# HGRN2 attention and FNet mixing on one core: the up-projection of three batches as fifteen block products in place of eighteen

## The chip, the cores and the metric

The kernel runs on one core of one Trainium2 chip. The core has five engines with an instruction queue each, which work side by side and wait for one another by semaphores: PE (TensorE, the matmuls; its weight loads are listed apart as PEld), DVE (VectorE), ACT (ScalarE), POOL (GpSimd) and SP (SyncE, which here only issues DMAs). Matmul results land in PSUM, which has eight banks; a bank holds 512 fp32 columns on 128 partitions. Everything else is in SBUF.

The metric is the device time of one execution in microseconds, lower is better. The time given is a median over several executions. A profile is one execution more, with the hardware profiler on.

## What is computed

The reference has two parts. The first is a gated linear recurrence over 768 steps for each of 4 batches and 8 heads with 48 channels. Its output `x` is a 768 x 384 matrix for each batch. The second part mixes it and applies a two-layer network:

```python
state = f[:, :, t, :, None] * state + np.einsum('bhd,bhe->bhde', k[:, :, t], v[:, :, t])
y[:, :, t] = np.einsum('bhd,bhde->bhe', q[:, :, t], state)
...
X = np.fft.fft(x, axis=1)
X = np.fft.fft(X, axis=2)
u = x + np.real(X)
mu = np.mean(u, axis=-1, keepdims=True)
var = np.mean((u - mu) ** 2, axis=-1, keepdims=True)
un = (u - mu) / np.sqrt(var + 1e-06)
ch = np.maximum(un @ w_ch1, 0.0) @ w_ch2
return u + ch
```

`w_ch1` is 384 x 1536 and `w_ch2` is 1536 x 384. The product `un @ w_ch1` is called the up-projection here, the product with `w_ch2` the down-projection. All matmuls of both are fp32.

## The kernel before

**Order of the work.** The order is written out by hand. `ORDER` (lines 27 to 47) is a string of words, and the loop at the end of the kernel issues one step for each word, so every engine's queue gets its instructions in the order of the words. A number `n` is the next step of attention unit `n`. There are 16 units, one for each pair of heads: units 0 to 3 belong to batch 0, and so on. `Ln` with letters loads a unit's f, k, q or v. `Kn` transposes a unit's keys. `Fb` is the next step of batch `b`'s Fourier mixing. `Hb` is the next step of its normalization and transposes. `Pb` is the next step of its two projections. `r` fetches a block of the weights, `C` converts it to fp32. `W` combines blocks of `w_ch2`. `V` and `c` read the weights a second time and look at their sizes. `D` are matmuls on constants during the start, and `M` computes a flag at the end. If that flag is set, a second and slower path computes everything again. With these inputs it isn't taken.

**Attention.** A unit's f, k and q (112 partitions x 768) live in one of four `g` tiles, one of three `k` tiles and one of four `q` tiles, picked by the unit's number (`u % 4`, `u % 3`, `u % 4`). A unit's steps are: two activations (lines 331, 332), a scan on DVE (338), exponentials (342 to 346), two products on DVE (350, 351), matmuls into a PSUM tile `sc` (359), a masked copy (363), matmuls into `y` (517), a second `sc` tile (534), state differences `ds` (557), a scan (565), matmuls into `y` (574), copies, transposes `yt` (594), and additions and subtractions on DVE that prepare the Fourier mixing, the fold (621 to 627). All these short-lived PSUM tiles come from the pool `ps_a`, which has two buffers of two banks each.

**Mixing and normalization.** `fnet` makes `z` (683) and `mix` (702), adds `mix` to `x` and takes the moments on DVE (line 758 and following). `turn` normalizes a tile of 128 tokens (738), transposes it on PE (741) and copies it to `unT` on ACT (742).

**Projections.** `projected` handles a batch in three pairs of token tiles. For each pair, `unT` holds 384 channels of two tiles of 128 tokens. The up-projection computes 12 blocks of 128 hidden channels. Each is three matmuls (one for each 128 channels, line 783) with 128 x 128 weights and 256 moving columns, the two token tiles side by side, into a buffer of the PSUM pool `ps_f`. ACT then applies the ReLU into `h` (785). `h` is kept in two tiles of six blocks each, from a pool `ph1` of two buffers. The down-projection then takes seven products of six matmuls each (806) in place of eight, with sums of `h` formed on DVE (813 to 824) and its results added to `x` on DVE (817 to 840). The first pair of batch 0 uses a plain down-projection (792), because the weights' combinations aren't ready by then. A step of `Pb` is one block of the up-projection or one of the seven products, so a pair takes 20 steps.

Of the kernel before, what the change touches and what calls it, by code (L numbers as in the profile page):

```python
# [12 lines left out]
C = 128  # L13
# [11 lines left out]


ORDER = (
    "L0f Z L1f I 0 D D L0q D 0 i D 1 1 D 0 L2f L0k 0 D D D r L0v D D C L1q D 2 D L2k 0 D L1k D 1 0 2 1 r "
    "0 L2q K0 C L3fk 0 D 0 1 2 D 1 2 3 0 3 2 2 L4fk L1v 4 K1 r 1 4 C 1 1 L3q 3 0 1 L2v K2 3 r 2 L3v 1 0 3 "
    "C 2 L5fk 3 D 5 D D 2 4 L4qv 2 R K3 2 3 1 D 3 4 2 3 4 3 2 5 L5qv 4 3 L7fk T 5 4 3 S K4 7 D 3 L6fk C r "  # L30
    "4 4 C F0 r F0 F0 5 F0 C 4 F0 K5 5 H0 5 H0 C r 4 5 H0 L7qv C r C r r F0 L6qv 6 F0 5 C P0 6 C P0 P0 P0 "
    "5 r 6 P0 P0 5 6 C 6 K6 r C P0 r H0 C 6 r P0 P0 P0 7 r C P0 6 r H0 C r P0 6 C 7 H0 r P0 C r 7 6 C r C "
    "P0 7 6 7 K7 r P0 L9fk L8qv C L9qv 7 C 6 L8fk C 7 5 P0 9 4 5 9 P0 P0 7 8 P0 P0 9 P0 P0 8 8 L10fk P0 9 "
    "7 9 L10qv K9 H0 P0 P0 8 P0 9 P0 P0 P0 9 8 9 H0 9 L11fk P0 W P0 9 K8 8 10 P0 11 10 P0 11 8 7 P0 8 6 "
    "11 P0 P0 P0 6 L11qv P0 11 P0 P0 8 10 P0 P0 7 P0 P0 P0 7 F1 F1 L13qv P0 F1 10 L13fk K10 F1 P0 10 10 8 "
    "L12fk F1 P0 10 11 L14fk H1 H1 P0 P0 12 F1 P0 10 H1 P0 P0 14 P0 P0 L12qv 10 12 P0 P0 12 P0 P0 P0 P1 "
    "P1 12 9 P1 P1 F1 11 10 K11 P1 P1 P1 H1 P1 P1 11 12 11 H1 P1 L15fk 11 13 P1 P1 14 10 11 8 13 13 H1 8 "
    "12 P1 P1 P1 P1 P1 10 P1 P1 P1 P1 P1 P1 11 9 K12 P1 13 10 P1 P1 P1 P1 P1 V P1 P1 H1 11 12 13 11 12 H1 "
    "P1 F2 12 F2 14 P1 P1 P1 P1 13 15 L14qv P1 P1 12 K13 P1 P1 F2 F2 P1 P1 14 13 14 F2 P1 13 H2 13 P1 V "
    "15 14 P1 P1 P1 P1 L15qv P1 H2 P1 P1 13 H2 F2 P1 15 14 K14 F2 P1 P1 P1 V P1 P1 P1 15 P1 P1 P2 H2 P2 "  # L40
    "P2 c V P2 c c P2 P2 P2 V V K15 P2 14 12 P2 P2 14 14 15 H2 P2 V c P2 15 c 12 15 14 P2 15 H2 P2 P2 15 "
    "13 c P2 P2 14 P2 c P2 H2 V 15 P2 H2 P2 P2 P2 13 14 V P2 P2 15 P2 V 15 15 P2 P2 P2 F3 P2 c F3 P2 F3 "
    "F3 P2 F3 F3 P2 F3 c c P2 P2 P2 P2 P2 P2 P2 P2 P2 V P2 P2 c P2 P2 P2 V c P2 H3 V P2 P2 H3 H3 P2 P2 P2 "
    "P2 P2 P2 P2 P2 P2 P2 P3 P3 P3 V V P3 V H3 c H3 V P3 P3 P3 c P3 c V c c V P3 H3 P3 P3 P3 P3 P3 V P3 c "
    "P3 V V c P3 V P3 c P3 P3 P3 c P3 P3 P3 P3 P3 H3 H3 P3 P3 P3 c P3 P3 P3 P3 P3 V P3 P3 P3 P3 P3 P3 P3 "
    "P3 P3 P3 c P3 P3 P3 c M P3 P3 P3 P3 P3 P3 P3 P3 P3 P3 P3 P3 P3"
)

PAIRS = ((0, 3), (2, 5), (1, 4))
LAST_PAIRS = ((2, 5), (1, 4), (3, 0))  # L50
# [3 lines left out]
def kernel(  # L54
# [32 lines left out]
    p2 = ctx.enter_context(tc.tile_pool(name="p2", bufs=2))  # L87
    pr = ctx.enter_context(tc.tile_pool(name="pr", bufs=3))
    p3 = ctx.enter_context(tc.tile_pool(name="p3", bufs=4))
    ph1 = ctx.enter_context(tc.tile_pool(name="ph1", bufs=2))  # L90
    ps_a = ctx.enter_context(tc.tile_pool(name="ps_a", bufs=2, space=bass.MemoryType.PSUM))
    ps_y = ctx.enter_context(tc.tile_pool(name="ps_y", bufs=1, space=bass.MemoryType.PSUM))
    ps_f = ctx.enter_context(tc.tile_pool(name="ps_f", bufs=2, space=bass.MemoryType.PSUM))
# [6 lines left out]

    nc.scalar.preload_act_table_set("natural_log_exp_and_others")

    g_t = [fixed([128, S + 1], f"g{i}") for i in range(4)]
    k_t = [fixed([128, S], f"k{i}") for i in range(3)]
    q_t = [fixed([128, S], f"q{i}") for i in range(4)]
    at_t = [fixed([128, 2, NCH, 64], f"at{i}") for i in range(2)]
    ao_t = [fixed([128, 2, NCH // 2, 64], f"ao{i}") for i in range(2)]
    causal = fixed([128, C], "causal")
# [48 lines left out]
    def load(u, *names):  # L157
        if u >= B * HP:
            return
        b, hp = divmod(u, HP)  # L160
        for name in names:
            if name == "v":
                v_of[u] = (p3.tile([128, NCH, 2 * D], F32, tag="v", name=f"v{u}"),
                           pr.tile([128, NCH // 2, 2 * D], F32, tag="vx", name=f"vx{u}"))
                nc.sync.dma_start(out=v_of[u][0], in_=v[b, hp])
                nc.sync.dma_start(out=v_of[u][1][64:], in_=v[b, hp, :64, 3:])
                continue
            t, i = {"f": (g_t[u % 4], 2), "k": (k_t[u % 3], 1), "q": (q_t[u % 4], 0)}[name]
            rows = qkf.rearrange("b h r d i s -> (b h r d) i s")
            first = 2 * D * u  # L170
            nc.sync.dma_start(out=t[:2 * D, :S], in_=rows[first:first + 2 * D, i])
            nc.sync.dma_start(out=t[2 * D:R, :S], in_=rows[first + D:first + 64, i])
# [116 lines left out]

    def reread():  # L290
        i = len(second)
        t = (k_t[1], g_t[1], k_t[2], g_t[2])[i % 4][:, :S].bitcast(U32)
        _, src, cols = blocks_of[i]
        if wide:
            nc.sync.dma_start(out=t, in_=src.bitcast(U32)[:, 2 * cols.start:2 * cols.stop])
        second.append(t.rearrange("p (n w) -> p n w", w=2))
# [27 lines left out]
    def attention(u, x_all):  # L324
# [1 line left out]

        Q, K, g = q_t[u % 4][:R], k_t[u % 3][:R], g_t[u % 4][:R, :S]
        AT, AO = at_t[u % 2], ao_t[u % 2]  # L330
        nc.scalar.activation(g, g, AF.Exp, scale=-1.0, accum_out=hot[:R, u:u + 1])
        nc.scalar.activation(g, g, AF.Ln, bias=1.0)  # L332
# [3 lines left out]
        T = deep[:R, u]  # L336
        W = p2.tile([128, S], F32, tag="W", name=f"W{u}")[:R]
        nc.vector.tensor_tensor_scan(W, g, bound[:R], 0.0, ALU.add, ALU.min)  # L338
        nc.vector.tensor_tensor(T, g_t[u % 4][:R, C::C], W[:, C - 1::C], ALU.add)
        yield  # L340

        nc.scalar.activation(g, W, AF.Exp, scale=-1.0)
# [26 lines left out]
    def attention_by_blocks(u, x_all):  # L369
# [2 lines left out]

        Q, K, g = q_t[u % 4][:R], k_t[u % 3][:R], g_t[u % 4][:R, :S]
        AT = ph1.tile([128, 2, NCH, C], F32, tag="h1", name=f"at{u}")
        nc.gpsimd.memset(AT, 0.0)
        masks = causal.rearrange("p (i n) -> p i n", n=32)
        AD = ph1.tile([128, 2, 2 * NCH, 64], F32, tag="h1", name=f"ad{u}")[:, :, :NCH, :32]
        nc.gpsimd.memset(AD, 0.0)  # L380
        mul = nc.vector.tensor_tensor

# [278 lines left out]
    def fnet(b, x):  # L661
# [94 lines left out]
        for c in range(3):  # L756
# [6 lines left out]
                nc.vector.tensor_copy(x[0:1, 3], row[0:1])  # L763
            yield

    def projected(b, x, again=False):


# [3 lines left out]
        for j, (c, d) in enumerate(PAIRS if b < B - 1 else LAST_PAIRS):  # L772
# [1 line left out]
                for _ in range((3, 3, 2)[j] if b < B - 1 else (3, 2, 3)[j]):  # L774
                    next(behind[b], None)
            unT = turned_of[b][j].rearrange("p k t n -> p k (t n)")
            hs = []
            for m in range(NF):
                if m % H == 0:
                    hs.append(ph1.tile([128, H, 2, 128], F32, tag="h1", name=f"h1_{b}_{j}_{m}"))  # L780
                pp = ps_f.tile([128, 512], F32, tag="f", name=f"up{b}_{j}_{m}")
                for kt in range(3):
                    nc.tensor.matmul(pp[:, :256], lhsT=w1[:, kt, m * 128:(m + 1) * 128], rhs=unT[:, kt],  # L783
                                     start=(kt == 0), stop=(kt == 2))
                nc.scalar.activation(hs[-1][:, m % H].rearrange("p t n -> p (t n)"), pp[:, :256], AF.Relu)  # L785
                yield
            if not again and (b, j) == (0, 0):

                for t, i in enumerate((c, d)):
                    po = ps_f.tile([128, 512], F32, tag="f", name=f"po{b}_{i}")  # L790
                    for m in range(NF):
                        nc.tensor.matmul(po[:, :DM], lhsT=hs[m // H][:, m % H, t], rhs=w2[:, m],  # L792
                                         start=(m == 0), stop=(m == NF - 1))
                        if m in (2, 5, 8):
                            yield
                    tt(x[:, i], po[:, :DM], x[:, i], ALU.add)
                    store(b, i, x[:, i])
                    yield
                continue
            h11, h21, h12, h22 = [hs[k][:, :, t] for k in range(2) for t in range(2)]  # L800
            c1, c2, d1, d2 = [x[:, i, o:o + HD] for i in (c, d) for o in (0, HD)]

            def product(i, out, h, start=False):
# [64 lines left out]
    with tc.manual_schedule():  # L868
        for word in ORDER.split():
# [3 lines left out]
                    units[n] = attention(n, lambda b=n // HP: x_all(b))  # L873
                next(units[n], None)
            elif kind == "K":
                keys_turned(n, g_t[n % 4][:R, :S])
            elif kind == "F":
                if n not in fronts:
                    fronts[n], rest[n] = fnet(n, x_of[n]), projected(n, x_of.pop(n))
# [2 lines left out]
                next(rest[n], None)  # L882
            elif kind == "W":
                combine()
            elif kind == "H":
                next(behind[n], None)
            elif kind == "r":
                fetch()
            elif kind == "V":
                reread()  # L890
            elif kind == "D":
                busy()
            elif kind == "C":
                weights()
            elif kind == "c":
                sizes()
            elif kind == "R":
                fetch(3)
            elif kind == "L":
                load(n, *word.strip("L0123456789"))  # L900
            elif kind == "I":
                start()
            elif kind == "i":
                nc.sync.dma_start(out=ident, in_=ident_in)
            elif kind == "T":
                wave = tables()
            elif kind == "S":
                sort_tables(wave)
            elif kind == "Z":
                zeros()  # L910
            elif kind == "M":
                flag = judge()
    tc.no_sync_barrier()
    again = nc.values_load(flag[0:1, 0:1], min_val=0, max_val=1)
    with tc.If(again > 0):
        if wide:
            for i, (dst, _, _) in enumerate(blocks_of):
# [86 lines left out]
```

## Time and profile before

| | |
|---|---|
| median of 3 executions | 542.58 us (542.5 to 543.71) |
| the profiled execution | 542.37 us |
| its span, from the first instruction to the last | 540.6 us |
| mean granted TensorE clock | 0.983 of full speed |
| PE busy with up-projection matmuls (L783) | 194.4 us, 864 records |
| PE busy with down-projection matmuls (L806), its five groups added | 161.8 us |
| DVE busy, ACT busy | 291.9 us, 201.1 us |
| DMA | 48.07 MB, mean 89 GB/s |

How to read it: an engine's busy time is the time in which at least one of its instructions runs, and "L783" is line 783 of the kernel. An fp32 matmul shows as two records on PE, each with a weight load of its own. Matmuls are pipelined: a record's length includes the way through the array, so the pace of a stream is read from how many records a stretch holds, not from their lengths. A group's line gives busy time and the mean length of one in ns, and then the engine's idle time ahead of the group and what ended it.

### The profile page before, as it was taken

To read this page: it belongs to the slowest core of one execution; us is meant where nothing else is said; L and a number is where in the kernel's file an instruction comes from. 1 tells how busy PE (TensorE), PEld (TensorE's weight loads), DVE (VectorE), ACT (ScalarE), POOL (GpSimd) and SP (SyncE) were. 2 spreads that over 40 slices of the span, in tenths; PEclk is the share of its full clock that TensorE was granted. 3 is DMA by queue.
4 is the path that set the end of the run, shared out by engine and by line. 5 is a ranking of instruction groups with operands and counts; after the bars stand their busy time and mean duration, and the time that the engine had idled before them with its cause. 6 is when DMAs were issued, how large, how long until landed. Compare 5 with 4: busy or idle time off the path is not lost.

```text
span 540.6 us, 12660 instructions
## 1 busy us (share of the span) xinstructions
PE 513.1 (95%) x5422; PEld 454.4 (84%) x5422; DVE 291.9 (54%) x559; ACT 201.1 (37%) x529; POOL 56.3 (10%) x85
## 2 busy tenths in 40 slices
PE   6787989989999999999999999999999999999995
PEld 6676778757898899899898899899889898989894
DVE  4878889958397344378442554255473142513231
ACT  6774757646362443352233341422311303021110
POOL 3110544431001000000001000000001000010000
PEclk9879889999999999999999999999999999999999
DMA  8997275588220320101201302204101007200001
GB/s 238 242 271 210 65 212 166 170 238 217 60 72 29 105 80 31 43 11 45 70 0 48 95 2 63 85 1 147 29 24 37 0 18 246 86 32 1 31 1 35
DMA packets 20455, 48.07 MB, mean 89 GB/s; under 512 B 3365, under 2 KB 5990, under 8 KB 20390
## 3 DMA queue, kind: packets, MB, share of 16 engines
q1 hardware_dynamic: 19142, 43.43, 28.2%
q0 software_dynamic: 1104, 3.54, 1.8%
q8 instruction: 44, 0.72, 0.6%
q14 instruction: 21, 0.17, 0.1%
q10 hardware_dynamic: 144, 0.20, 0.1%
HBM read 42.44 MB, written 4.72 MB: 87 GB/s over the span
## 4 chain that ended last, share of the span: by engine, by line
PE 82%; DVE 7%; DMA 5%; POOL 2%; issue 2%; ACT 1%; SPq 0%; DVEq 0%; POOLq 0%
PE up L783 32%; PE fx L806 16%; PE fz L806 12%; DMA raw<-in_w_ch_dram 3%; PE y L517 3%; PE z L683 3%; PE mix L702 2%; PE ds L557 2%; PE sc L359 2%; PE y L574 2%; PE y L151 2%; DMA wave<-in_dim_tab_dram 2%; PE po L792 2%; PE yt L594 1%; PE pt L741 1%
## 5 line engine op out<-in xcount | busy, mean ns | idle before, releaser
L783 PE MATMUL up<-unT,w 128*128 128x256 f32 x864 | 194.4, 380 | 0.4 <-DVE x L761 0.2
L783 PEld LDWEIGHTS up<-unT,w 128*128 128x128 f32 x864 | 161.4, 190 | 22.4 <-ACT h L785 0.7
L785 ACT ACTIVATE h<-up 128x256 f32<-128x256 f32 x144 | 55.2, 384 | 183.3 <-PE up L783 170.7
L650 POOL DMA_INDIRECT out_dram<-x,place x16 | 17.1, 1070 | 399.6 <-DVE x L836 298.1
L806 PE MATMUL fx<-block,h 128*128 128x192 f32 x264 | 46.6, 326 | 0.0
L806 PE MATMUL fx<-w,h 128*128 128x192 f32 x264 | 45.3, 326 | 0.7 <-DVE x L761 0.7
L806 PEld LDWEIGHTS fx<-w,h 128*128 128x128 f32 x264 | 43.2, 190 | 1.3 <-PE mix L702 0.9
L806 PEld LDWEIGHTS fx<-block,h 128*128 128x128 f32 x264 | 43.3, 190 | 0.1
L565 DVE TENSOR_TENSOR_SCAN stt<-ds,te 112x288 f32<-112x288 f32 x16 | 12.0, 751 | 38.7 <-PE ds L557 38.7
L338 DVE TENSOR_TENSOR_SCAN W<-g,bound 112x768 f32<-112x768 f32 x16 | 28.1, 1757 | 8.2 <-ACT g L332 8.2
L244 POOL TENSOR_TENSOR w<-w,raw 128x384 uint32<-128x384 uint32 x24 | 26.2, 1094 | 57.2 <-DVE w L243 32.0
L813 DVE TENSOR_TENSOR s<-h,h 128x768 f32<-128x768 f32 x11 | 10.5, 952 | 38.5 <-ACT h L785 38.5
L806 PE MATMUL fz<-block,h 128*128 128x192 f32 x132 | 23.4, 327 | 0.1
L806 PE MATMUL fz<-w,s 128*128 128x192 f32 x132 | 23.3, 326 | 0.0
L806 PE MATMUL fz<-w,h 128*128 128x192 f32 x132 | 23.2, 326 | 0.0
L363 DVE COPY_PREDICATED at<-causal,sc 128x768 f32<-128x768 uint32 x16 | 16.5, 1033 | 11.3 <-PE sc L359 11.3
L806 PEld LDWEIGHTS fz<-block,h 128*128 128x128 f32 x132 | 21.6, 190 | 0.5 <-PE fx L806 0.3
L806 PEld LDWEIGHTS fz<-w,h 128*128 128x128 f32 x132 | 21.8, 190 | 0.0
L806 PEld LDWEIGHTS fz<-w,s 128*128 128x128 f32 x132 | 21.7, 190 | 0.0
L742 ACT COPY unT<-pt 128x384 f32<-128x384 f32 x24 | 11.6, 483 | 24.5 <-PE pt L741 24.4
L517 PEld LDWEIGHTS y<-at,v 64*48 64x48 f32 (+1 forms) x768 | 15.5, 136 | 6.1 <-issue 2.7
L517 PE MATMUL y<-at,v 64*48 64x64 f32 (+1 forms) x768 | 19.1, 231 | 1.5 <-DVE at L363 1.0
(146 smaller groups left out, 750.3 us busy)
## 6 DMA issues: line engine op xcount, KB each, us to landing
raw<-in_w_ch_dram SPq DMA_DIRECT2D x24, 384.0 KB
g<-in_qkf_dram SPq DMA_DIRECT2D x16, 288.0 KB
q<-in_qkf_dram SPq DMA_DIRECT2D x16, 288.0 KB
k<-in_qkf_dram SPq DMA_DIRECT2D x16, 288.0 KB
v<-in_v_dram SPq DMA_DIRECT2D x16, 288.0 KB
k<-in_w_ch_dram SPq DMA_DIRECT2D x12, 384.0 KB
g<-in_w_ch_dram SPq DMA_DIRECT2D x12, 384.0 KB
vx<-in_v_dram SPq DMA_DIRECT2D x16, 72.0 KB
```

Of the source, the lines that this page charges most:

```text
L151: nc.tensor.matmul(spare, lhsT=bound[:, :C], rhs=bound[:, :C], start=not started, stop=True, skip_group_check=True)
L244: nc.gpsimd.tensor_tensor(bits, bits, lo, ALU.add)
L338: nc.vector.tensor_tensor_scan(W, g, bound[:R], 0.0, ALU.add, ALU.min)
L363: nc.vector.copy_predicated(AT, causal[:, :64].bitcast(U32).unsqueeze(1).unsqueeze(1).to_broadcast([128, 2, NCH, 64]), own[:, :, :NCH * 64 ...
L517: nc.tensor.matmul(y[FILL[g], c // 3, c % 3 * C + t.start:c % 3 * C + t.stop], lhsT=vals[rows, o:o + (64 if g == 0 else D)], rhs=weights, ...
L565: nc.vector.tensor_tensor_scan(flat(st[:R]), ps[:R, 0, :NCH * D], flat(te), 0.0, ALU.add, ALU.mult)
L650: nc.gpsimd.indirect_dma_start(out=out.rearrange("b s d -> (b s) d"), out_offset=bass.IndirectOffsetOnAxis(ap=place[:, b, i:i + 1], axis=0 ...
L683: nc.tensor.matmul(z[:, cols], lhsT=src[:, j, lo:hi], rhs=tab[:, t, T % 2, cols], start=(i == 0), stop=(i == len(parts) - 1), skip_group_c ...
L742: nc.scalar.copy(turned[j][:, :, t], pt[:, :DM].rearrange("p (k t) -> p k t", k=3))
L783: nc.tensor.matmul(pp[:, :256], lhsT=w1[:, kt, m * 128:(m + 1) * 128], rhs=unT[:, kt], start=(kt == 0), stop=(kt == 2))
L785: nc.scalar.activation(hs[-1][:, m % H].rearrange("p t n -> p (t n)"), pp[:, :256], AF.Relu)
L806: nc.tensor.matmul(out, lhsT=h[:, m], rhs=blocks[i][:, m], start=(start and m == 0), stop=(m == H - 1), skip_group_check=True)
```

## The change

The up-projection of batches 1 to 3 is a product of a 2 x 3 arrangement of token blocks (two token tiles, three groups of 128 channels) with a 3 x 3 arrangement of weight blocks (three groups of 128 channels, three groups of 512 hidden channels). Written plainly it has 2 x 3 x 3 = 18 block products. The change computes it with 15 block products on sums and differences of blocks. Batch 0 keeps the plain form.

- `WEIGHTS`: sixteen sums or differences of 128 x 512 weight blocks, one for each word `B` in the new list, on DVE (`weight_sum`). Six new blocks lie in `extra`, each made in one or two steps; the others replace blocks of `w1` in place.
- `PRODUCTS`: for each pair of token tiles, ten sums or differences of 128 x 128 token blocks on DVE, in `sums` or in place in `unT`; fifteen products of four matmuls with 128 moving columns each; and fifteen evictions of a whole bank (128 x 512): six by ACT as a copy, with a sign, into `h`, and nine by DVE, which adds them to `h` or subtracts them from it. Some products accumulate on what their bank still holds after an eviction. Six ReLUs on ACT then work in place in `h`.
- The two banks of a pair are one tile of the pool `ps_a`, named `sc`, held from the first product to the last. A step of `Pb` in these batches is one product, so a pair takes 23 steps.
- `extra` and `sums` share memory (`wide_t`) with the tiles `g2`, `g3`, `k2`, `q2` and `q3`. From unit 8 on, units use only the sets 0 and 1 (`home`).
- `h` is one tile of twelve blocks from a pool of one buffer. The second read of the weights uses `k_t[0]` and `g_t[0]` in place of `k_t[2]` and `g_t[2]`.
- `ORDER` is a new list throughout, from the first loads on.

The core of the diff, without the list:

```diff
+PRODUCTS = (
+    (((6, 1, 4, '+'), (7, 6, 0, '+')), 3, 0, 0, True, 3, '=+', False),
+    (((8, 2, 6, '-'),), 4, 5, 1, True, 5, '=+', False),
+    (((9, 1, 0, '+'),), 7, 9, 0, True, 0, '=-', False),
+    (((10, 1, 2, '-'),), 8, 13, 1, False, 2, '=-', False),
+    (((11, 8, 5, '+'), (4, 11, 3, '-'), (1, 4, 0, '-'), (7, 2, 1, '-')), 9, 3, 0, False, 2, '-', False),
+    ((), 10, 12, 1, False, 1, '=-', False),
+    (((8, 4, 10, '+'),), 7, 2, 0, False, 5, '+', False),
+    ((), 11, 7, 1, False, 4, '=+', False),
+    ((), 8, 10, 0, False, 3, '-', True),
+    ((), 5, 11, 1, True, 5, '+', True),
+    ((), 4, 6, 0, False, 4, '+', True),
+    ((), 6, 4, 1, True, 1, '+', False),
+    ((), 1, 1, 0, False, 1, '-', True),
+    ((), 2, 8, 1, False, 2, '+', True),
+    ((), 0, 14, 0, False, 0, '+', True),
+)
+WEIGHTS = (
+    (9, 3, 6, 'n'), (10, 2, 6, '-'), (11, 8, 2, '+'), (12, 5, 10, '-'), (12, 12, 4, '-'), (13, 12, 6, '-'),
+    (13, 13, 7, '-'), (14, 9, 0, '+'), (14, 14, 1, '+'), (0, 6, 0, '+'), (4, 7, 4, '+'), (8, 13, 8, '+'),
+    (3, 3, 10, '-'), (7, 7, 1, '+'), (5, 3, 5, '+'), (6, 6, 1, '-'),
+)
+FLIP = 1
...
-    ph1 = ctx.enter_context(tc.tile_pool(name="ph1", bufs=2))
+    ph1 = ctx.enter_context(tc.tile_pool(name="ph1", bufs=1))
...
+    def home(name, u):
+        if few[0] and u >= 2 * HP:
+            u %= 2
+        return {"f": g_t[u % 4], "k": k_t[u % 3], "q": q_t[u % 4]}[name]
...
+    def add(to, one, two, sign):
+        if sign == "n":
+            nc.vector.scalar_tensor_tensor(to, one, -1.0, two, ALU.mult, ALU.subtract)
+        else:
+            nc.vector.tensor_tensor(to, one, two, ALU.add if sign == "+" else ALU.subtract)
+    def weight_sum():
+        to, one, two, sign = WEIGHTS[summed[0]]
+        add(block(to), block(one), block(two), sign)
+        summed[0] += 1
+    def hidden(name, unT, h):
+        tokens = lambda i: unT[:, i % 3, i // 3 ^ FLIP] if i < 6 else sums[:, i - 6]
+        banks = ps_a.tile([128, 2, 512], F32, tag="sc", name=name)
+        for made, a, w, bank, new, to, how, complete in PRODUCTS:
+            for i, one, two, sign in made:
+                add(tokens(i), tokens(one), tokens(two), sign)
+            for m in range(4):
+                nc.tensor.matmul(banks[:, bank, m * 128:(m + 1) * 128], lhsT=block(w)[:, m * 128:(m + 1) * 128],
+                                 rhs=tokens(a), start=(new and m == 0), stop=True, skip_group_check=True)
+            out = h[:, to % 3 * 4:to % 3 * 4 + 4, to // 3 ^ FLIP]
+            got = banks[:, bank].rearrange("p (m n) -> p m n", n=128)
+            if how[0] == "=":
+                nc.scalar.activation(out, got, AF.Copy, scale=1.0 if how == "=+" else -1.0)
+            else:
+                nc.vector.tensor_tensor(out, out, got, ALU.add if how == "+" else ALU.subtract)
+            if complete:
+                nc.scalar.activation(out, out, AF.Relu)
+            yield
...
+            h = ph1.tile([128, NF, 2, 128], F32, tag="h1", name=f"h1_{b}_{j}")
+            if b and not again:
+                yield from hidden(f"ub{b}_{j}", turned_of[b][j], h)
+            for m in range(NF if again or not b else 0):
```

## The prediction

> **What bounds the kernel now.** I read the page first: busy shares, then the forty slices.
>
> ```profile
> span 540.6 us, 12660 instructions
> PE 513.1 (95%) x5422; PEld 454.4 (84%) x5422; DVE 291.9 (54%) x559; ACT 201.1 (37%) x529; POOL 56.3 (10%) x85
> ...
> PE   6787989989999999999999999999999999999995
> ...
> DVE  4878889958397344378442554255473142513231
> ```
>
> From the ninth slice on (about 110 us) TensorE is full. Before that, loads, weight conversion and VectorE share the bound. So a microsecond taken from PE after 110 us counts, unless another engine's queue becomes the limit. Next, the costliest groups:
>
> ```profile
> L783 PE MATMUL up<-unT,w 128*128 128x256 f32 x864 | 194.4, 380 | 0.4 <-DVE x L761 0.2
> L783 PEld LDWEIGHTS up<-unT,w 128*128 128x128 f32 x864 | 161.4, 190 | 22.4 <-ACT h L785 0.7
> L785 ACT ACTIVATE h<-up 128x256 f32<-128x256 f32 x144 | 55.2, 384 | 183.3 <-PE up L783 170.7
> ```
>
> The up-projection is the largest item, and it waits for nobody (0.4 us idle in all). An fp32 matmul is two records: 432 matmuls give 864. Then the stages: P0's last two pairs (125 to 210), and samples of P2 and P3.
>
> ```profile
> 125.00:165.00 40.00, 40.00 (x544) 35.63 (x543) 29.50 (x44) 21.40 (x48) 2.24 (x1) 1.00 0.35 93
> 165.00:210.00 45.00, 45.00 (x456) 40.32 (x454) 23.26 (x48) 17.11 (x51) 2.93 (x3) 1.00 0.23 64
> ...
> 372.00:413.00 41.00, 40.19 (x219) 35.54 (x218) 20.57 (x49) 10.21 (x39) 1.71 (x2) 1.00 0.17 57
> 413.00:443.00 30.00, 29.85 (x161) 27.59 (x161) 9.20 (x19) 5.91 (x16) 1.91 (x2) 1.00 0.04 14
> ```
>
> Columns are length, then busy PE, PEld, DVE, ACT, POOL, the granted clock (1.00 is full), the DMA share and GB/s. PE is full; DVE (third value) is at half through P1 and P2 and at a third in P3. That spare DVE time is what the change spends.
>
> **Price of a 128-column matmul.** The trace has no fp32 matmul of 128 columns on a 128x128 block. The chain of waits gives cadences by count:
>
> ```profile
> 172.56 2.60 PE z L683 x12
> ...
> 176.46 1.32 PE z L683 x8
> ...
> 412.98 12.96 PE up L783 x60
> ...
> 429.69 3.90 PE fx L806 x24
> ```
>
> 256 columns: 12.96/60 = 0.216 us a record. 192 columns: 3.90/24 = 0.1625. A line through these gives 0.109 at 128. The z groups test whether weight loads spoil it: six records of 385, 193 and 192 columns take 1.30, eight with 385, 97, 96 and 192 take 1.32, so a 96- or 97-column record behind a load as wide costs (0.02 + 2 x 0.163)/4 = 0.0865, against 0.083 on the line; scaled by 128/97 that is 0.114. I take 0.112, nearer the z row, and keep 0.109 and 0.114. The 190 ns of a load record is no bound: in z, load records of 163 ns follow each other every 87.
>
> The Trainium skill, TensorE: Matmul & The Clock Gate, Back-to-back issue gap, speaks against the change: in streams where every matmul has its own weight load it gives about 81 ns at N=128 against 56 for the matmul alone. Carried over to two passes (my estimate) a record would be 0.162, a pair 19.4 us, and the kernel some 35 us slower. The z row disagrees, 0.0865 against that rule's 45% surcharge, so I don't use it.
>
> **Part by part.**
>
> *Removed and added on PE*, per pair of token tiles in P1 to P3 (nine pairs): out go 36 matmuls, 72 x 0.216 = 15.55 us; in come 15 products x 4 = 60, 120 x 0.112 = 13.44. That is -2.11 a pair, -19.0 in all (bounds -22.2 at 0.109, -16.8 at 0.114).
>
> *Evictions.* A product fills a whole bank (128x512); the two banks alternate, so product n+2 waits for the eviction of product n, covered only by product n+1 (8 x 0.112 = 0.90 us). The latency is read here:
>
> ```profile
> 425.77 1.18 PE L741 MATMUL pt<-ident,un 128*128 128x128 f32 x6
> ...
> 426.30 0.48 ACT L742 COPY unT<-pt 128x384 f32<-128x384 f32 x1
> ...
> 426.83 0.91 PE L783 MATMUL up<-unT,w 128*128 128x256 f32 x3
> 426.99 0.48 ACT L742 COPY unT<-pt 128x384 f32<-128x384 f32 x1 [0.21 <-PE pt L741]
> ```
>
> PE's last transpose ends at 426.95, ACT starts 0.04 later. The first copy ends at 426.78, the matmul that waits for it starts 0.05 later. Three matmul records then take 0.91 where a stream takes 2 x 0.216 + 0.38 = 0.81: 0.10 to start up. A 128-column record ends 0.16 after its slot (0.27 long, as the flag's matmul at L862). Loop: 0.16 + 0.04 + 0.05 + 0.10 = 0.35 plus the eviction. Eviction on DVE from two rows:
>
> ```profile
> L836 DVE TENSOR_TENSOR x<-fz,x 128x192 f32<-128x192 f32 x11 | 3.9, 356 | 11.1 <-PE fz L806 11.0
> ...
> L796 DVE TENSOR_TENSOR x<-po,x 128x384 f32<-128x384 f32 x2 | 1.1, 544 | 2.1 <-PE po L792 2.1
> ```
>
> 188 ns per 192 columns, so 0.67 at 512. On ACT 384 ns at 256 (L785) and 483 at 384 (L742) give 0.58. The loop is 1.02 on DVE and 0.93 on ACT against 0.90: a stall of 0.12 or 0.03 at every second product (the one between finds its eviction done). About five of the seven are DVE's: 0.65 a pair where nothing stands between products, in P3; half of it, 0.3, in P1 and P2, where attention's matmuls stand between many. Bounds 0 and, if both products stalled, 1.3.
>
> *DVE's queue.* Per pair ten 128x128 sums at 0.29 (0.36 at 192, 0.56 at 384 columns) and nine evictions at 0.67: 9.0 us. P1 and P2 (210 to 413) had 103.0 of 203; now 157 of about 190, 82%. P3 goes to about 55%. DVE is in order: a fold of a unit (2.4 us, L621 to L627), a scan (1.76) or normalization in front of an eviction holds PE, and behind PE's wait stand attention, transposes and products alike. I read the built DVE order for one bad place, P2's second pair: after `both` (0.2 + 0.56) and three sums (0.9), unit 15's fold (2.4) stands before the sum product 5 reads, ready at 4.4 where PE is there at 3.5: 0.9 late. Then five sums more hold product 5's eviction, so product 7 is 0.45 late. That pair loses 1.4; elsewhere in P1 and P2 gaps look filled by matmuls of attention. I take 1.1 a pair over six pairs; bounds 0 and 8 (the 49 us of DVE work of units 10 to 15, 8.1 a unit by their rows, all exposed). P3 has only L303's reductions (0.54) in between: 0.3 a pair.
>
> *ACT.* Per pair six copies at 0.58 and six ReLUs at 0.63 (112x768 takes 0.845, less 256 columns) replace twelve at 0.384: +2.7, ACT from 201 to 225 us. The ReLUs hold no product. The down-projection's first two products (3.9 us) read token tile 0, complete after product 11; they hide the last eviction, its ReLU and the sum s1.
>
> *Weight sums.* Sixteen 128x512 DVE sums at 0.69: 11 us in P0, where DVE had 52.8 of 85; P0's own matmuls wait on ACT only. I take +1, bounds 0 and 11.
>
> *Two tile sets from unit 8; one PSUM buffer.* Loads of unit u+2 wait until unit u has read its tiles; the trace's landings of the late loads are 3.0 to 6.2 us after issue. New order: five products (4.5 us) stand between load and first use for units 13 and 14, fewer for 15. If late, ACT waits at L331 with evictions queued behind. SP issues as many loads as before. The banks of a pair keep one of the two `sc` buffers, so attention steps in a pair follow one another through one buffer. Both I count inside the 1.1. The single `h1` buffer costs nothing: its first write waits for the last down-projection product, which precedes it on PE anyway.
>
> *Sum:* -19.0 + 3 x (0.65 + 0.3) + 6 x (0.3 + 1.1) + 1 = -6.8. The profiled execution took 542.37 (span 540.6 and 1.8 around it), 0.2 under the median of 542.58: forecast 536 for the median.
>
> **Rivals.** *Nearly all of it arrives:* the attention matmuls hide evictions and queue. For it: before, PE lost only 0.4 us at L783 with a similar interleaving. Against: P3 has nothing to interleave. -19.0 + 2 + 1: about 526.
>
> *DVE becomes the bound (slower).* Place: P1 and P2, 82% busy and in order. Break-even: 19.0 - 2.9 - 1 = 15.1, so 2.5 us lost in each of six pairs instead of 1.4. At 4 a pair, the time is 542.6 - 19.0 + 2.9 + 24 + 1 = 551. For it: the late place above is close to this already. Against: most long DVE operations in the order stand opposite attention's PE work.
>
> *Given back (no change):* the losses come to 17 to 20. About 542.5.
>
> *Narrow matmuls bring nothing* (a record at 0.13): the pair is 15.6 us, and the losses come on top: 555. The z row speaks against it; it goes with the slower case.
>
> **Numbers.** A measurement tells changes over 0.3%, 1.6 us. Forecast (530 to 541) 0.46; nearly all (under 530) 0.20; no change 0.07; slower 0.27. So faster 0.66, same 0.07, slower 0.27. The likeliest case's own range is 530 to 541; the range for 8 in 10 reaches to 521 (0.109 and half the losses) and 550 (DVE's case nearly whole).
>
> **What would show it.** Product records every 0.109 to 0.114, 0.27 long: if 0.13 or more, the price is wrong. In P3 a gap of about 0.1 at every second late product, released by DVE; pairs 29 us long against 30.4 before (the last L840 of P2 stands at 443.4, that of P3's first pair at 473.7). In P1 and P2 idle PE before the products of 1.4 a pair; above 2.5 I am wrong about DVE. ACT's wait at L331 over 10 us (8.4 before) would put the loss on the loads, and a later P1 start than 210 on the weight sums.

## The result and the profile after

The changed kernel takes 638.1 us (median of 4 runs, 632.3 to 641.4) against 542.7 for the kernel before on the same chip: a ratio of 1.174, 95% interval 1.166 to 1.183. The forecast was 536, its range ended at 550: wrong by a sign and by 102 us.

The page of the changed kernel, the lines that answer to those of before (shares, then the forty slices):

```profile
span 639.7 us, 13808 instructions
PE 535.2 (84%) x5854; PEld 476.0 (74%) x5854; DVE 379.4 (59%) x746; ACT 225.7 (35%) x529; POOL 53.6 (8%) x85
...
PE   6786898999999879879888889789679679679675
...
DVE  4588999785858755638456746745256324325242
...
PEclk8897999999999999999999999999989968958999
```

The tail was the fullest part of the kernel before; now it is among the emptiest: in the last nine slices, P3, where little but products and down-projections runs, the row of PE falls to 6 and 7, and the clock's row falls to 6 and 5. DVE did not become the bound: it has 2 to 5 tenths there.

The groups of the evictions (L843, L841), the products (L836, in four forms) and the ReLU (L845); then the waits (engine, what waited, for what; us in all, times, longest):

```profile
L843 DVE TENSOR_TENSOR h<-h,ub 128x512 f32<-128x512 f32 x81 | 55.6, 687 | 135.1 <-PE ub L836 134.9
L841 ACT ACTIVATE h<-ub 128x512 f32<-128x512 f32 x54 | 32.3, 597 | 121.6 <-PE ub L836 105.2
L836 PE MATMUL ub<-unT,w 128*128 128x128 f32 x360 | 56.4, 305 | 19.6 <-DVE h L843 14.6
...
L845 ACT ACTIVATE h<-h 128x512 f32<-128x512 f32 x54 | 34.0, 630 | 86.2 <-DVE h L843 86.2
L836 PE MATMUL ub<-wide,w 128*128 128x128 f32 x288 | 42.8, 293 | 21.8 <-DVE h L843 12.3
L836 PE MATMUL ub<-wide 128*128 128x128 f32 x288 | 41.2, 286 | 20.7 <-ACT h L841 15.0
...
L836 PE MATMUL ub<-unT,wide 128*128 128x128 f32 x144 | 22.4, 303 | 13.0 <-DVE h L843 13.0
```

```profile
PE ub L836 <- DVE h L843: 45.6, 57, 2.0
...
PE ub L836 <- ACT h L841: 29.3, 44, 0.7
...
ACT g L372 <- DMA g<-in_qkf_dram: 2.8, 2, 2.4
```

The up-projection waited 0.4 us before; now 101 of 135 products wait for an eviction, 75 us by this count. By the time from one product record to the next, beyond the 0.112 us that a record takes in a stream, it is 106 us: this also counts the start-up after a wait and some 8 us of records that ran at half clock (last section). The evictions wait for the products in turn (135 and 105 us): neither side is late, they take turns. The durations were close to the forecast: evictions 0.687 and 0.597 us (0.67 and 0.58), records 0.112 apart.

How they take turns, in a timeline of the last pair of P3 at full clock (start, length, engine and line; in brackets the idle time before it and what ended it):

```profile
596.82 1.16 PE L836 MATMUL ub<-wide 128*128 128x128 f32 x8 [0.69 <-ACT h L841]
598.01 0.60 ACT L841 ACTIVATE h<-ub 128x512 f32<-128x512 f32 x1 [1.25 <-PE ub L836]
...
598.66 1.16 PE L836 MATMUL ub<-wide,w 128*128 128x128 f32 x8 [0.69 <-ACT h L841]
599.93 0.69 DVE L843 TENSOR_TENSOR h<-h,ub 128x512 f32<-128x512 f32 x1 [3.47 <-PE ub L836]
...
600.67 1.16 PE L836 MATMUL ub<-wide 128*128 128x128 f32 x8 [0.85 <-DVE h L843]
601.87 0.60 ACT L841 ACTIVATE h<-ub 128x512 f32<-128x512 f32 x1 [3.26 <-PE ub L836]
...
602.51 1.16 PE L836 MATMUL ub<-wide,w 128*128 128x128 f32 x8 [0.69 <-ACT h L841]
```

The product at 598.66 starts 0.05 after the end (598.61) of the eviction of the product at 596.82: the one right before it, which lies in the *other* bank. The forecast had it wait for the one before that. The same holds for all 126 products that follow another in their pair: none starts less than 0.05 us after the end of the eviction right before it. So a product costs its eight slots, 0.89 us, plus a whole loop: 1.84 from start to start with ACT (loop 0.95, forecast 0.93), mostly 1.93 to 2.01 with DVE at full clock (1.04 to 1.12, forecast 1.02).

The pair's tile also takes one of its two `sc` buffers from attention. That isn't where PE lost time: in P1 and P2 it idles 44.6 us, all of it in front of products.

### The profile page after: what moved, and what is told of

It reads as the page before. It is cut to its first block, busy times and chain, and to the rows that moved or that the text cites. A ratio compares the mean times of both kernels' runs of the same rounds, so it can differ in the third digit from the quotient of the medians.

```text
span 639.7 us, 13808 instructions
## 1 busy us (share of the span) xinstructions
PE 535.2 (84%) x5854; PEld 476.0 (74%) x5854; DVE 379.4 (59%) x746; ACT 225.7 (35%) x529; POOL 53.6 (8%) x85
## 4 chain that ended last, share of the span: by engine, by line
PE 74%; DVE 11%; DMA 6%; ACT 5%; issue 2%; SPq 1%; POOL 0%; DVEq 0%; ACTq 0%
PE ub L836 24%; PE fx L888 14%; PE fz L888 10%; DVE h L843 6%; PE up L865 5%; ACT h L841 4%; PE z L725 3%; PE y L559 3%; PE mix L744 2%; PE po L874 2%; PE sc L400 2%; PE pt L783 2%; PE y L616 2%; PE ds L599 2%; DMA wave<-in_dim_tab_dram 1%
## 5 line engine op out<-in xcount | busy, mean ns | idle before, releaser
L843 DVE TENSOR_TENSOR h<-h,ub 128x512 f32<-128x512 f32 x81 | 55.6, 687 | 135.1 <-PE ub L836 134.9
L841 ACT ACTIVATE h<-ub 128x512 f32<-128x512 f32 x54 | 32.3, 597 | 121.6 <-PE ub L836 105.2
L836 PE MATMUL ub<-unT,w 128*128 128x128 f32 x360 | 56.4, 305 | 19.6 <-DVE h L843 14.6
L836 PEld LDWEIGHTS ub<-unT,w 128*128 128x128 f32 x360 | 49.4, 211 | 25.6 <-DVE h L843 18.7
L845 ACT ACTIVATE h<-h 128x512 f32<-128x512 f32 x54 | 34.0, 630 | 86.2 <-DVE h L843 86.2
L836 PE MATMUL ub<-wide,w 128*128 128x128 f32 x288 | 42.8, 293 | 21.8 <-DVE h L843 12.3
L836 PE MATMUL ub<-wide 128*128 128x128 f32 x288 | 41.2, 286 | 20.7 <-ACT h L841 15.0
L836 PEld LDWEIGHTS ub<-wide,w 128*128 128x128 f32 x288 | 36.1, 197 | 28.2 <-DVE h L843 15.3
L836 PEld LDWEIGHTS ub<-wide 128*128 128x128 f32 x288 | 35.0, 191 | 26.7 <-ACT h L841 19.4
L865 PE MATMUL up<-unT,w 128*128 128x256 f32 x216 | 49.4, 381 | 0.6 <-ACT unT L784 0.6
L865 PEld LDWEIGHTS up<-unT,w 128*128 128x128 f32 x216 | 40.2, 190 | 6.3 <-ACT unT L784 0.8
L836 PE MATMUL ub<-unT,wide 128*128 128x128 f32 x144 | 22.4, 303 | 13.0 <-DVE h L843 13.0
L836 PEld LDWEIGHTS ub<-unT,wide 128*128 128x128 f32 x144 | 19.2, 206 | 16.1 <-DVE h L843 16.1
```

The lines of the kernel that those rows point to most:

```text
L836: nc.tensor.matmul(banks[:, bank, m * 128:(m + 1) * 128], lhsT=block(w)[:, m * 128:(m + 1) * 128], rhs=tokens(a), start=(new and m == 0), ...
L841: nc.scalar.activation(out, got, AF.Copy, scale=1.0 if how == "=+" else -1.0)
L843: nc.vector.tensor_tensor(out, out, got, ALU.add if how == "+" else ALU.subtract)
L845: nc.scalar.activation(out, out, AF.Relu)
```

## The experiments

Lengths in us by stage, from the start of one pair's last down-projection record to that of the next, taken from the profiled executions (P0 from the start of the span); the time is the median of all runs. The changed kernel's profiled execution was its slowest, 641.4.

| kernel | time | P0 ends | P1 and P2 | P3's three pairs |
|---|---|---|---|---|
| before | 542.6 | 209.6 | 233.4 | 30.4, 30.3, 30.0 |
| after | 638.1 | 211.2 | 283.6 | 48.1, 47.8, 41.9 |
| e1_two | 538.0 | 212.4 | 229.3 | 30.0, 28.8, 29.1 |
| e2_plain | 556.6 | 213.4 | 241.5 | 33.0, 30.4, 30.1 |
| e3_onetile | 600.6 | 212.3 | 265.1 | 39.6, 37.4, 37.9 |
| e4_head | 535.4 | 208.9 | 230.6 | 29.9, 28.8, 29.1 |

**Two tiles in place of one (e1_two).**

```diff
-        banks = ps_a.tile([128, 2, 512], F32, tag="sc", name=name)
+        banks = [ps_f.tile([128, 512], F32, tag="f", name=f"{name}_{i}") for i in range(2)]
+        held[0] = True
...
-                nc.tensor.matmul(banks[:, bank, m * 128:(m + 1) * 128], lhsT=block(w)[:, m * 128:(m + 1) * 128],
+                nc.tensor.matmul(banks[bank][:, m * 128:(m + 1) * 128], lhsT=block(w)[:, m * 128:(m + 1) * 128],
...
+        if held[0]:
+            return ps_a.tile([128, 2, 512], F32, tag="sc", name=name)[:, 0]
+        return ps_f.tile([128, 512], F32, tag="f", name=name)
```

> The changed kernel with the two banks of a pair as two tiles of their own from ps_f instead of one two-bank tile of ps_a; while a pair holds them, the scratch tiles of z, mix, mid and pt come from ps_a, and one P2 word stands ahead of the first P3 word. Products, sums, evictions, weight sums, two tile sets and (but for that word) the list are the changed kernel's. Theory A (in one tile each product waits for the eviction of the product right before it, about 0.85 to 1.0 us at each of 135 products; in two tiles product n+2 waits for eviction n, as my forecast priced it): 536 us, between 528 and 552; the idle time of PE between successive products falls from 107 us to under 30. Rival B (the sums and evictions in VectorE's queue, the two tile sets or the list cost the time by themselves): stays above 600. Between 552 and 600: both have a part.

Measured: 538.0 us, ratio 0.989 (0.982 to 0.996). Same products, evictions, sums; 100 us less than the changed kernel. Its page and the timeline of a late stretch of a pair in P3 (here the products are L843, ACT's evictions L848, DVE's L850):

```profile
PE 501.6 (94%) x5854; PEld 459.1 (86%) x5854; DVE 377.6 (70%) x746; ACT 224.7 (42%) x529; POOL 53.2 (10%) x85
```

```profile
480.06 1.16 PE L843 MATMUL ub<-wide 128*128 128x128 f32 x8
...
481.05 1.06 PE L843 MATMUL ub<-unT,wide 128*128 128x128 f32 x8
481.25 0.69 DVE L850 TENSOR_TENSOR h<-h,ub 128x512 f32<-128x512 f32 x1 [1.25 <-PE ub L843]
...
482.00 1.16 PE L843 MATMUL ub<-unT,w 128*128 128x128 f32 x8
482.20 0.69 DVE L850 TENSOR_TENSOR h<-h,ub 128x512 f32<-128x512 f32 x1 [0.26 <-PE ub L843]
...
482.99 1.11 PE L843 MATMUL ub<-wide,w 128*128 128x128 f32 x8
483.19 0.69 DVE L850 TENSOR_TENSOR h<-h,ub 128x512 f32<-128x512 f32 x1 [0.30 <-PE ub L843]
```

The eviction at 481.25 (of the product at 480.06) runs beside the product at 481.05; the product at 482.00 starts 0.06 after it ends. That is the loop as forecast: n+2 waits for n. Products are 0.95 to 0.99 apart against 0.89 in a stream, and 108 of the 126 products start before the eviction right before them has ended. The time lost between product records falls from 106 to 6 us, as much as the kernel gains. Theory A holds, rival B falls. (e1_two takes its tiles from another pool, which moves some scratch tiles too; e3_onetile below leaves those where they are.)

**The same list without products (e2_plain).**

```diff
-            if b and not again:
-                yield from hidden(f"ub{b}_{j}", turned_of[b][j], h)
-            for m in range(NF if again or not b else 0):
+            for m in range(NF):
...
                 yield
+                if b and not again and m % 4 == 3:
+                    yield
...
             elif kind == "B":
-                weight_sum()
+                pass
```

> The changed kernel's list, two tile sets and single h tile, with the up-projection of batches 1 to 3 as in the kernel before: twelve blocks of three 256-column matmuls over the fifteen steps, and without the weight sums. Theory A: list and tile sets cost little, 540 to 550. Rival B in its form 'two tile sets or the list': above 560, with the wait in front of the exponentials of the units (ACT on loads) over 10 us.

Measured: 556.6 us, ratio 1.022 (1.017 to 1.026). Theory A's range was missed: the list costs 13 us, where the expectation had at most 7. Not by the loads: no wait of ACT for them comes near 10 us (3.7 at L372). Against this kernel, its true control, e1_two is 18.6 us faster.

P1 with P2, and P3, in the view of stretches (length, then busy PE, PEld, DVE, ACT, POOL; first before, then e2_plain, then e1_two):

```profile
209.60:443.00 233.40, 231.18 (x2059) 208.88 (x2058) 112.21 (x236) 68.67 (x205) 8.07 (x9) 1.00 0.14 42
443.00:533.70 90.70, 90.24 (x485) 83.27 (x483) 27.82 (x59) 16.06 (x42) 3.92 (x5) 1.00 0.19 62
```

```profile
213.40:454.90 241.50, 235.42 (x2216) 209.55 (x2216) 114.28 (x238) 74.21 (x213) 7.91 (x9) 1.00 0.20 62
454.90:548.40 93.50, 91.55 (x491) 83.99 (x489) 26.55 (x58) 16.92 (x44) 3.93 (x5) 1.00 0.14 43
```

```profile
212.40:441.70 229.30, 223.70 (x2505) 212.71 (x2504) 164.62 (x355) 89.55 (x213) 8.56 (x9) 1.00 0.21 64
441.70:529.60 87.90, 87.20 (x635) 85.21 (x633) 52.18 (x115) 24.97 (x44) 3.93 (x5) 1.00 0.16 51
```

In P1 and P2 PE idles 2.2 us before (233.40 less 231.18), 6.1 in e2_plain and 5.6 in e1_two. (By the gaps between records, which also count waits that the tail of a record covers, it is 7.4, 14.0 and 14.7.) So the extra idle time there belongs to the list, and not to DVE's work: e1_two adds 50 us of that to the stage (114 to 165) and PE idles no more. The single `h` tile came with the list and isn't tested apart; P3's last two pairs have it too and take as long as before (30.4 and 30.1 against 30.3 and 30.0). The new list also moves matmuls of attention from P0 into P1 and P2 (2216 records against 2059), while P0 ends 3.8 later, not earlier.

**One tile without products (e3_onetile).** If one tile is the cause, a plain up-projection must suffer from it too.

```diff
+            if b and not again:
+                banks = ps_a.tile([128, 2, 512], F32, tag="sc", name=f"ub{b}_{j}")
             for m in range(NF):
-                pp = ps_f.tile([128, 512], F32, tag="f", name=f"up{b}_{j}_{m}")
+                if b and not again:
+                    pp = banks[:, m % 2]
+                else:
+                    pp = ps_f.tile([128, 512], F32, tag="f", name=f"up{b}_{j}_{m}")
```

> The kernel with the list, the tile sets and the plain up-projection again, but its twelve blocks of a pair go by turns into the two banks of one tile of ps_a instead of a new tile of ps_f each; no products, no sums, every eviction on ScalarE at about 0.38 us. Theory A: each of 108 blocks waits for the eviction of the block before it, 0.35 + 0.38 = 0.73 us where nothing stands between, so 27 us in P3 and up to 52 more in P1 and P2: 580 to 625. Rival B (VectorE's queue): within 6 us of the same kernel with a tile for each block, since VectorE has nothing more to do.

Measured: 600.6 us, inside theory A's range and 44 more than e2_plain (ratio to before 1.106, 1.100 to 1.112). P3 of this kernel (blocks L868, ReLU L870):

```profile
561.11 1.56 PE L868 MATMUL ub<-unT,w 128*128 128x256 f32 x6 [0.47 <-ACT h L870]
562.71 0.38 ACT L870 ACTIVATE h<-ub 128x256 f32<-128x256 f32 x1 [1.65 <-PE ub L868]
...
563.14 1.56 PE L868 MATMUL ub<-unT,w 128*128 128x256 f32 x6 [0.47 <-ACT h L870]
```

A block every 2.03 us, of which six records of 0.216 are 1.30: a loop of 0.73, the very figure expected. No sums, no product, no more DVE work: the shared tile does it. In P3, where no attention needs the other buffer, 21 us of the 44 are lost (114.9 against 93.5).

**The head of the list (e4_head, e5_plainhead).** Up to the loads of unit 9 the list of before, then the changed list without the words already done; e4_head is e1_two with it, e5_plainhead e2_plain. The first line of the list in both:

```diff
-    "L0f I D D L1f D L0k D 0 D i L0q D D D L2f L0v L1k D 0 1 0 D L1q D 1 1 2 0 Z L3fk 0 0 L1v 2 D L2q D D L2k "
+    "L0f Z L1f I 0 D D L0q D 0 i D 1 1 D 0 L2f L0k 0 D D D r L0v D D C L1q D 2 D L2k 0 D L1k D 1 0 2 1 r 0 "
...
```

> The kernel with two tiles for the banks, and the head of the list (up to the loads of unit 9) as in the kernel before; what follows is the changed kernel's list without the words already done. In the changed list PE lost 36 us of the first 100 and reached the last token tile of P0's first pair 6 to 8 us later than before (107.6 to 109.6 against 101.4). Theory C (the head of the new list costs this, the products don't): 528 to 533, P0's first pair ends near 125. Rival D (what follows was laid out for its own head, so the gain is lost behind it): 536 to 542.

> The kernel with the changed list and the plain up-projection, with the same exchange of the head. Theory C: 6 to 8 us less than its 556.6, so 547 to 551; the remaining 5 to 8 over the kernel before stand in P1 and P2 and come from the list behind the head. Rival D: 554 or more.

Measured: 535.4 us (ratio 0.985, 0.981 to 0.989) and 553.7 us (1.019, 1.014 to 1.024): 3 us less each (e4_head than e1_two, e5_plainhead than e2_plain; their runs spread over 2 to 7 us, so the 3 is rough), between the two theories. P0's first pair ends at 127.5 (131.0 in e1_two), yet only about 3 us reach the end. The head costs about 3 us of the 13; e4_head is the fastest kernel of this study, 8 us faster than the kernel before.

**Two tile sets or the order of the words (e7_sets).** e5_plainhead with as many tile sets as before.

```diff
-    few = [True]
+    few = [False]
...
-        t = (k_t[1], g_t[1], k_t[0], g_t[0])[i % 4][:, :S].bitcast(U32)
+        t = (k_t[1], g_t[1], k_t[2], g_t[2])[i % 4][:, :S].bitcast(U32)
```

> The kernel with the plain up-projection, the changed list and the head of before, but with the four, three and four tile sets of the kernel before for every unit in place of two from unit 8 (possible here, since no sums take their place). It tells the two tile sets from the order of the words. Its fellow with two sets: 553.7, PE idle 14.6 us in P1 and P2 against 7.4 before. Theory E (the order of the words loses it): 552 to 555. Rival F (the late loads of two sets lose it): 545 to 549, idle in P1 and P2 near 8.

The list was laid out for two sets; with four, tiles of some units (keys at least) are overwritten by a later unit's load before the unit's last steps, so part of attention is computed from other numbers, by the same instructions. Measured: 552.5 us against 553.7, ratio to before 1.020 (1.015 to 1.025). P1 and P2 are as long, with nearly the same idle PE (6.1 and 6.2); e7_sets, then e5_plainhead:

```profile
209.10:451.40 242.30, 236.22 (x2222) 210.32 (x2221) 114.77 (x239) 74.22 (x213) 8.32 (x9) 1.00 0.20 62
```

```profile
209.10:451.40 242.30, 236.12 (x2217) 209.76 (x2217) 114.41 (x238) 74.26 (x213) 7.99 (x9) 1.00 0.20 62
```

Theory E's range holds: the tile sets don't lose it. That leaves the order of the words, by elimination; no run changes it alone behind the head.

## Why the prediction was wrong

The 95.4 us between before and after (each against its own runs of before) are made up of three parts: the list, e2_plain less before, +13.0; the products with two tiles, e1_two less e2_plain, -18.6; one tile in place of two, the rest, +101.0, of which some 12, in the profiled execution, are matmuls at half clock (last section).

*The step that failed* is, in the prediction's words, "the two banks alternate, so product n+2 waits for the eviction of product n, covered only by product n+1 (0.90 us)". The loop was priced about right, 0.93 and 1.02 against 0.95 and 1.04 to 1.12. What it was set against was wrong: there is no cover. Both banks belong to one tile, and each product waits for the eviction right before it, whichever bank that reads (126 of 126 in the trace); with a tile for each bank it doesn't (e1_two). So the waits go by the tile. The prediction read the built order, but not for which instruction each product waits. With 0.93 x 54 + 1.02 x 81 = 133 us as the whole of the loops, less what attention and the down-projection hide, the same rows would have given the right sign. The Trainium skill's PSUM — Partial Sum Buffer (PSUM bank collisions raise a hardware error) says that TensorE and another engine must not touch the same bank at once. That asks for an order within a bank; nothing in it asks for one between two banks, and e1_two's trace shows a product and an eviction side by side in two banks (481.05 and 481.25).

*Removed and added on PE*, -2.11 a pair: right. Records came 0.112 apart, the figure taken. P3's last two pairs are 28.8 and 29.1 in e1_two, forecast 29, and e2_plain's are 30.4 and 30.1. (That the trace before has no fp32 matmul of this width on such a block is not so: the transposes of its own fence, L741, are that, and come 0.109 apart where they stream.)

*The rest of evictions*, 0.65 a pair in P3 and 0.3 in P1 and P2: about right once there are two tiles. The stall is 0.05 to 0.12 at nearly every late product, not 0.12 at every second. The time lost between products is 1.0 a pair in P3, where 0.65 and 0.3 for DVE's queue were forecast, and 0.5 in P1 and P2.

*DVE's queue*, 1.1 a pair in P1 and P2, and the rival that it becomes the bound: neither shows. PE idles 5.6 us with the sums and evictions in the queue and 6.1 without. The 82% was too high: it put the work of six pairs into a stretch (210 to 413) that leaves out P2's last pair. By the row of before above, 112 and 54 more make 166 of some 220, 75%; e1_two has 165 of 229, 72%. What the bad place in P2's second pair costs by itself wasn't tried. That e1_two landed 2 us from the forecast is in part luck: this term and the weight sums were too dear, and the list's cost was not in the sum at all.

*Weight sums*, +1: they cost nothing that shows. P0 ends at 212.4 with them (e1_two) and at 213.4 without (e2_plain). The prediction named a late start of P1 (211.2 after) as their sign; the list is late without them, so the sign was no test.

*Two tile sets*: right, free. After the change ACT waits 2.8 us for loads at L372 (8.4 before, at the same step, L331), and four sets gain e7_sets no more than 1.2 us, within the spread of its runs.

*What the sum left out*: the rewritten list, +13.0. The prediction counted instructions added and moved but took the kernel before as the control for the order of all the others. 3 us of it are the head; the rest stands in P1, P2 and the first pair of P3. Which words lose it stays open.

*The rivals*: "nearly all of it arrives" had the products right and missed the tile. The slower case named DVE, with 551. None named the tile; the range could not hold 638. (Its lower end, 521, doesn't follow from the terms that it names either: 542.6 less 22.2, with half of the 12.2 us of losses, is 526.5.)

## What to carry to other kernels

In these runs two banks overlapped only where they were two tiles. Before pricing a double buffer, read for which instruction the second writer waits, and if both halves lie in one tile, price the whole loop. When a change rewrites a hand-made order as well, the kernel before is not its control: run the new order with the old computation, or count the order as a cost of its own (13 us of 543 here, as large as two thirds of the gain). A loop of known length that appears 135 times deserves both prices, covered and uncovered, in the range.

## What the runs showed of the hardware

The granted clock fell to half in the later part of the changed kernel, though PE was never idle for over 2.0 us there. Two stretches of its P3 and one of the last pair (the value after the five engines is the granted clock):

```profile
517.80:531.40 13.60, 11.26 (x44) 10.38 (x43) 5.13 (x7) 2.03 (x4) 0.00 (x0) 0.50 0.10 29
562.30:579.20 16.90, 13.78 (x53) 12.61 (x53) 5.78 (x8) 2.84 (x5) 0.00 (x0) 0.50 0.00 1
600.00:613.00 13.00, 7.70 (x54) 6.55 (x55) 3.57 (x6) 3.09 (x5) 0.00 (x0) 1.00 0.00 0
```

```profile
519.81 2.08 PE L836 MATMUL ub<-unT,w 128*128 128x128 f32 x8 [0.78 <-DVE h L843]
522.66 2.07 PE L836 MATMUL ub<-unT,w 128*128 128x128 f32 x8 [0.78 <-DVE h L843]
```

A product then comes every 2.85 us in place of 1.95. The last 4 us of each of the two stretches hold the start of a down-projection, whose first 24 records take 5.9 us in place of 3.9. P3's first two pairs take 48.1 and 47.8, the third, all at full clock, 41.9: together 12.1 us are lost. Two shorter falls (3.4 us each) are earlier. The runs go with it: 632.3 us at a mean granted clock of 0.972, 641.4 at 0.953. So the waits were in part paid a second time, by matmuls that ran slower. A stream that is busy for 0.89 us of 1.84 to 2.01 fell to half; e3_onetile, busy for 1.30 of 2.03, and e1_two did not between 90 us and the end of their last pair. What sets off a fall isn't shown: the third pair had the same pace and kept the full clock.

The Trainium skill, TensorE: Matmul & The Clock Gate, A second HAM failure mode: psum-queue depth-cycling, tells of such falls where PE idles often and briefly between groups of matmuls. The changed kernel agrees; e3_onetile, which also waits at its blocks, shows none. The page's Part 1 speaks of one whole idle window of about 3.4 us; the falls here last about 3.4 us or multiples of it (3.4, 3.4, 13.7, 17.1), but no idle time of that length stands before them: in the 10 us ahead of each, PE's longest was 0.85 us, and 2.0 in one case.
